# Split first loads, reassigned fill work, idle matmuls and later row sums in a fused attention and feed-forward kernel

## Chip, cores, metric

One core of one Trainium2 chip. The time is the device time of one execution in microseconds; medians are over the runs that the tables count. The engines go by their short names: PE is TensorE (PEld its weight loads), DVE VectorE, ACT ScalarE, POOL GpSimd, SP SyncE, which only issues loads and stores here. The granted clock is the share of the full clock, as a run's records give it. PE is called cold at a granted clock of 0.50, and warm at 1.00; where no clock is on record, the time of a matmul tells (a dn matmul took 548 ns in the first group of the kernel before and 349 in its long part).

## The reference

```python
# q, k, v: (8, 12, 448, 64) float32; w_in: (768, 2048); w_out: (2048, 768); alpha: (2048,)
q_n = q / sqrt(mean(q*q, -1) + 1e-6) * g_q
k_n = k / sqrt(mean(k*k, -1) + 1e-6) * g_k
attn = softmax(q_n @ k_n^T / 8)
x = (attn @ v), heads side by side            # (3584, 768)
h = x @ w_in
out = (max(h, 0) + alpha * min(h, 0)) @ w_out # (3584, 768) float32
```

## The kernel before

Heads go through in 24 groups of four (y; three groups in each of 8 batches). The program is a list of blocks n; each makes two score tiles and their exponentials, and in some blocks also the denominators (`den`, matmul group dn), the weighted values (`attv`, av, written to xT), or the transposes (`turn`, tps, copied out to qT and kT) of a group. From block 12 on, the gaps of the blocks are filled with feed-forward work: `up` (matmuls hT, then ah on ACT, then gT on DVE) and `down` (matmuls op, then osb). In the traces of this case an engine's work runs in the order of this list (two row sums at 107.11 us run ahead of the gT that PE waits for, shown below), so where a call stands decides what it holds up. The code is abridged:

```python
def load_qk(y):
    b, i = divmod(y, G)
    for nm in "qk":
        t = ld.tile([128, 2, J, D], FP32, name="nat", tag="nat", bufs=6)
        eng = nc.scalar if y < 2 and nm == "k" else nc.sync
        for g in range(2):                       # g: half of the partitions
            eng.dma_start(out=t[ds(64 * g, 64)]..., in_=SRC[nm][b, g, :, ds(2 * i, 2)])
        nat[y, nm] = t

def square(y, nm):    # sq = nat * nat: ACT for y == 0, else POOL (1.68 us); two buffers
def reduce(y, nm):    # ss = row sums of sq: DVE, 1.08 us
def root(y):          # rr = exp(-0.5 * ln(ss / D + eps)): ACT, 0.54 us
def scale(y, nm):     # qs = nat * rr
    eng = nc.vector if y == 0 or (y < G and nm == "q") else nc.gpsimd
...
# later groups, n = 3.5 y
at(n - 6, square, y, nm); at(n - 5, reduce, y, nm); at(n - 4, root, y); at(n - 3, scale, y, nm)
...
# the fill
for nm in "qk":
    square(0, nm); reduce(0, nm); root(0, nm); scale(0, nm)
turn(0)
for y in (1, 2):
    for nm in "qk":
        square(y, nm)
        at(0, reduce, y, nm) if y == 2 else reduce(y, nm)
at(1, root, 1); at(2, root, 2)
for nm in "qk":
    at(1, scale, 1, nm); at(2, scale, 2, nm)
load_v(0)
for c in range(4):
    at(2, load_w_in, c)
...
for n in range(NB + 2):
    for f, a in prep.get(n, ()):      # what at() put there: the front of the block
        f(*a)
    # scores; den or attv; exponentials; turn; the gap's ups and downs
```

Of the kernel before, what the change touches and what calls it, by code (L numbers as in the profile page):

```python
# [9 lines left out]
FP32 = mybir.dt.float32  # L10
FP16 = mybir.dt.float16
# [10 lines left out]
def kernel(  # L22
# [12 lines left out]
    nc = tc.nc  # L35

    B, H, S, D = q.shape
# [4 lines left out]
    G = HH // 2  # L42
# [7 lines left out]
    cst = ctx.enter_context(tc.tile_pool(name="cst", bufs=1))  # L50
# [5 lines left out]
    psf = ctx.enter_context(tc.tile_pool(name="psf", bufs=2, space=bass.MemoryType.PSUM))  # L56
# [15 lines left out]
    nc.vector.memset(ones, 1.0)  # L72
    ident = cst.tile([128, 128], FP16, name="ident", tag="ident")
    make_identity(nc, ident)
    gain = cst.tile([128, 1], FP32, name="gain", tag="gain")
    gk2 = cst.tile([128, 1], FP32, name="gk2", tag="gk2")
    alpha_sb = cst.tile([128, NF], FP32, name="alpha_sb", tag="alpha_sb")
# [8 lines left out]
    def load_qk(y):  # L86
        b, i = divmod(y, G)
        for nm in "qk":
            t = ld.tile([128, 2, J, D], FP32, name="nat", tag="nat", bufs=6)
            eng = nc.scalar if y < 2 and nm == "k" else nc.sync  # L90
            for g in range(2):
                eng.dma_start(
                    out=t[ds(64 * g, 64)].rearrange("p h j d -> p h (j d)"),
                    in_=SRC[nm][b, g, :, ds(2 * i, 2)],
                )
            nat[y, nm] = t

    def load_v(b):
        t = att.tile([128, HH, J, D], FP16, name="vt", tag="vt")
        for g in range(2):  # L100
            nc.gpsimd.dma_start(
                out=t[ds(64 * g, 64)].rearrange("p h j d -> p h (j d)"), in_=v4[b, g]
            )
        vt[b] = t

    def load_w_in(c):
        nc.gpsimd.dma_start(
            out=w_in_sb[:, :, ts(c, FB)],
            in_=moe_w_in[:, ts(c, FB)].rearrange("(k p) f -> p k f", p=128),
        )  # L110
# [8 lines left out]
    def square(y, nm):  # L119
        src = nat[y, nm].rearrange("p h j d -> p (h j d)")  # L120
        sq = ld.tile([128, 2 * J, D], FP32, name="sq", tag="sq", bufs=2)
        sqf = sq.rearrange("p n d -> p (n d)")
        if y == 0:
            nc.scalar.activation(out=sqf, in_=src, func=AF.Square)  # L124
        else:
            nc.gpsimd.tensor_mul(out=sqf, in0=src, in1=src)  # L126
        sqs[y, nm] = sq

    def reduce(y, nm):
        if nm == "q":  # L130
            ss_t[y] = ld.tile([128, 2, 2, J], FP32, name="ss", tag="ss", bufs=4)
        nc.vector.tensor_reduce(  # L132
            out=ss_t[y][:, "qk".index(nm)].rearrange("p h j -> p (h j)").unsqueeze(2),
            in_=sqs[y, nm], axis=AXIS_X, op=ALU.add,
        )

    def root(y, nms="qk"):
        n = len(nms)
        at = "qk".index(nms[0])
        if at == 0:  # L140
            rr_t[y] = ld.tile([128, 2, 2, J], FP32, name="rr", tag="rr", bufs=4)
        rr, ss = rr_t[y][:, ds(at, n)], ss_t[y][:, ds(at, n)]
        nc.scalar.activation(out=rr, in_=ss, func=AF.Ln, scale=1.0 / D, bias=epsb[:, 0:1])
        nc.scalar.activation(out=rr, in_=rr, func=AF.Exp, scale=-0.5)  # L144

    def scale(y, nm):
        t = ld.tile([128, J, 2, D], FP16, name="qs", tag="qs", bufs=4)
        eng = nc.vector if y == 0 or (y < G and nm == "q") else nc.gpsimd
        eng.tensor_mul(  # L149
            out=t.rearrange("p j h d -> p h j d"),  # L150
            in0=nat[y, nm],
            in1=rr_t[y][:, "qk".index(nm)].unsqueeze(3).broadcast_to((128, 2, J, D)),
        )
        qs[y, nm] = t

    def turn(y):

        ps = psa.tile([128, 2, 512], FP32, name="tps", tag="acc")
        tps = [
            ps[:, n, : S].bitcast(FP16).rearrange("p (j c) -> p j c", j=J)  # L160
            for n in range(2)
        ]
        for tp, nm in zip(tps, "qk"):
            for j in range(J):
                nc.tensor.transpose(  # L165
                    tp[:, j, :], qs[y, nm][:, j].rearrange("p h d -> p (h d)"), ident
                )
        for tp, nm in zip(tps, "qk"):
            t = att.tile([128, 2, J, 64], FP16, name=f"{nm}T", tag=f"{nm}T", bufs=3)
            o = t.rearrange("p g j c -> p j g c")  # L170
            i4 = tp.rearrange("p j (g c) -> p j g c", g=2)
            if nm == "q":
                nc.vector.tensor_copy(out=o, in_=i4)  # L173
            else:
                nc.vector.tensor_scalar(  # L175
                    out=o, in0=i4, scalar1=gain[:, 0:1], scalar2=None, op0=ALU.mult
                )
            qkT[y, nm] = t
# [4 lines left out]
    def score(y, j):  # L183
        qT, kT = qkT[y, "q"], qkT[y, "k"]
        sc = pss.tile([128, 2, 512], FP32, name="sc", tag="sc")
        for par in range(2):
            for g in range(2):
                nc.tensor.matmul(  # L188
                    out=sc[ds(64 * g, 64), par, :S],
                    lhsT=kT[ds(64 * par, 64), g, j, :],  # L190
                    rhs=qT[ds(64 * par, 64), g].rearrange("p j c -> p (j c)"),
                    start=True,
                    stop=True,
                )
        scs[y, j] = sc
# [24 lines left out]
    def den(y):  # L220
        dn = over_keys("dn", y, lambda g, par, j: ones[ds(64 * g, 64), :])
        rden[y] = dn

    def log(y):
        r = att.tile([128, 2, S], FP32, name="rden", tag="rden")
        nc.scalar.activation(out=r, in_=rden[y][:, :, :S], func=AF.Ln)  # L226
        rden[y] = r
# [33 lines left out]
    def down(b0, t, oh):  # L261
# [14 lines left out]
        if oh == 1:  # L276
            for half in range(2):
                bb, j = divmod(2 * t + half, J)
                nc.sync.dma_start(out=out4[b0 + bb, j], in_=o[ds(64 * half, 64)])




# [2 lines left out]
    def last(y):  # L286
        return (J * y + J - 1) // 2

    dens = {last(y) + 1: y for y in range(NG)}
    avs = {last(y) + 2: y for y in range(NG)}  # L290
    prep = {}

    def at(n, f, *a):
        prep.setdefault(max(int(n), 0), []).append((f, a))

    for y in range(G, NG):
        n = J * y / 2
        at(n - 12, load_qk, y)
        for nm in "qk":
            at(n - 6, square, y, nm)  # L300
            at(n - 5, reduce, y, nm)
        at(n - 4, root, y)
        for nm in "qk":
            at(n - 3, scale, y, nm)
    for b in range(1, B):
# [27 lines left out]
    def cost(n):  # L333
        return 0.75 + (1.35 if n in dens or n in avs else 0.0) + (0.9 if n in turns else 0.0)

    gaps = [[] for _ in range(NB + 2)]
    for b in range(B - 1):
        lo = last(G * b + G - 1) + 2
# [3 lines left out]
        n, clock, done = lo, cost(lo), 0.0  # L342
# [15 lines left out]
    load_qk(2)  # L358
    nc.sync.dma_start(out=alpha_sb, in_=moe_alpha.rearrange("(t p) -> p t", p=128))

    for nm in "qk":
        square(0, nm)
        reduce(0, nm)
        root(0, nm)
        scale(0, nm)
    nc.vector.tensor_mul(out=gain, in0=gain, in1=gk2)
    turn(0)
    for y in (1, 2):
        for nm in "qk":
            square(y, nm)  # L370
            at(0, reduce, y, nm) if y == 2 else reduce(y, nm)
    at(1, root, 1)
    at(2, root, 2)
    for nm in "qk":
        at(1, scale, 1, nm)
        at(2, scale, 2, nm)
    load_v(0)
    for c in range(4):
        at(2, load_w_in, c)
        at(8 + 2 * c, load_w_out, c)  # L380

    for n in range(NB + 2):
        for f, a in prep.get(n, ()):
            f(*a)
        tiles = [divmod(m, J) for m in (2 * n, 2 * n + 1) if m < NG * J]
        for t in tiles:
            score(*t)
        late = []
        if n in dens:
            den(dens[n])  # L390
        if n in avs:
            attv(avs[n])
        plain = n not in dens and n not in avs and n not in turns
        wait = plain and gaps[n] and gaps[n][0][0] is up
        for t in tiles[:1] if wait else tiles:
            soft(*t)
        if wait:
            late = [(soft, t) for t in tiles[1:]]
        if n in dens:
            log(dens[n])  # L400
            late = [(invert, (dens[n],))]
        if n in turns:
            turn(turns[n])
        for f, a in gaps[n]:
            f(*a)
            if f is up and late:
                for g, c in late:
                    g(*c)
                late = []
        for g, c in late:  # L410
            g(*c)
    for f, a in rest:
        f(*a)

# [29 lines left out]
```

## Time and profile before

| | before |
|---|---|
| median, 3 runs | 494.11 us (493.31 to 494.29) |
| span of the profiled run | 493.35 us (time of that run: 495.12) |
| first score's kT written / second group's kT written | 18.84 / 32.45 us |
| first full up-projection (hT after xT of batch 0) | 63.08 us |
| from there to the end | 430.27 us |

Read it as two stretches: a fill, in which engines wait for each other and for loads, and a long part, in which PE is nearly always busy. The prediction shows the lines that say so.

### The profile page before, as it was taken

To read this page: it belongs to the slowest core of one execution; us is meant where nothing else is said; L and a number is where in the kernel's file an instruction comes from. 1 tells how busy PE (TensorE), PEld (TensorE's weight loads), DVE (VectorE), ACT (ScalarE), POOL (GpSimd) and SP (SyncE) were. 2 spreads that over 40 slices of the span, in tenths; PEclk is the share of its full clock that TensorE was granted. 3 is DMA by queue.
4 is the path that set the end of the run, shared out by engine and by line. 5 is a ranking of instruction groups with operands and counts; after the bars stand their busy time and mean duration, and the time that the engine had idled before them with its cause. 6 is when DMAs were issued, how large, how long until landed. Compare 5 with 4: busy or idle time off the path is not lost.

```text
span 493.3 us, 9405 instructions
## 1 busy us (share of the span) xinstructions
PE 441.2 (89%) x4016; PEld 232.7 (47%) x4016; DVE 222.4 (45%) x312; ACT 287.4 (58%) x397; POOL 168.4 (34%) x124
## 2 busy tenths in 40 slices
PE   0447789999999999999999999999999999999995
PEld 0124344554445545554445555554445554454463
DVE  1781546534633535624633535634643543324421
ACT  2448878857675567557675566557675576523300
POOL 2696662535335325225335325325325200000000
PEclk9998799999999999999999999999999999999998
DMA  8599997317441470416341470417311110120122
GB/s 184 115 171 262 234 236 154 76 33 179 60 108 32 108 160 5 108 33 180 60 106 33 108 161 4 108 33 182 56 33 33 34 34 1 33 52 13 32 65 64
DMA packets 32186, 45.45 MB, mean 92 GB/s; under 512 B 5008, under 2 KB 28560, under 8 KB 32144
## 3 DMA queue, kind: packets, MB, share of 16 engines
q1 hardware_dynamic: 19792, 32.13, 25.2%
q0 software_dynamic: 11776, 11.80, 15.1%
q10 hardware_dynamic: 576, 0.92, 0.8%
q8 instruction: 31, 0.51, 0.5%
q14 instruction: 11, 0.09, 0.1%
HBM read 45.62 MB, written 11.01 MB: 115 GB/s over the span
## 4 chain that ended last, share of the span: by engine, by line
PE 67%; DVE 13%; ACT 12%; issue 4%; DMA 2%; POOL 1%; SPq 0%; DVEq 0%; POOLq 0%
PE op L265 29%; PE hT L248 19%; PE dn L211 7%; PE sc L188 6%; ACT ah L256 6%; PE av L211 5%; DVE gT L257 4%; ACT expT L200 4%; DVE ss L132 4%; DMA nat<-in_q_dram 2%; PE tps L165 2%; DVE qs L149 1%; DVE kT L175 1%; DVE qT L173 1%; POOL sq L126 1%
## 5 line engine op out<-in xcount | busy, mean ns | idle before, releaser
L200 ACT ACTIVATE expT<-sc,expb 128x896 f16<-128x896 f32 x168 | 160.2, 1003 | 59.1 <-PE sc L188 59.1
L248 PE MATMUL hT<-xT,w_in_sb 128*128 128x448 f16 x768 | 159.5, 352 | 13.0 <-DVE gT L257 11.9
L265 PE MATMUL op<-w_out_sb,gT 128*128 128x384 f16 x896 | 152.9, 326 | 0.2 <-DVE gT L257 0.2
L149 POOL TENSOR_TENSOR qs<-nat,rr 128x896 f16<-128x896 f32 x44 | 73.3, 1686 | 211.3 <-ACT rr L144 191.4
L256 ACT ACTIVATE ah<-hT,alpha_sb 128x448 f16<-128x448 f32 x128 | 81.3, 635 | 97.4 <-PE hT L248 96.1
L257 DVE TENSOR_TENSOR gT<-hT,ah 128x448 f16<-128x448 f32 x128 | 79.6, 624 | 108.4 <-ACT ah L256 107.8
L265 PEld LDWEIGHTS <-gT 128*128 128x128 f16 x896 | 85.0, 98 | 63.6 <-issue 10.1
L248 PEld LDWEIGHTS <-w_in_sb 128*128 128x128 f16 x768 | 72.3, 97 | 89.8 <-issue 30.1
L275 DVE COPY osb<-op 128x384 f32<-128x384 f32 x56 | 31.2, 557 | 115.3 <-PE op L265 115.3
L126 POOL TENSOR_TENSOR sq<-nat 128x896 f32<-128x896 f32 x46 | 76.3, 1678 | 12.9 <-DMA nat<-in_q_dram 8.6
L188 PE MATMUL sc<-qT,kT 64*64 64x448 f16 x672 | 53.5, 383 | 12.0 <-DVE kT L175 6.7
L132 DVE TENSOR_REDUCE ss<-sq 128x14 f32<-128x896 f32 x48 | 50.1, 1078 | 16.1 <-ACT sq L124 8.6
L165 PE MATMUL tps<-ident,qs 128*128 128x128 f16 x336 | 24.5, 227 | 20.3 <-DVE qs L149 20.3
L211 PE MATMUL dn<-expT,ones 64*64 64x448 f16 x672 | 39.8, 376 | 0.0
L211 PE MATMUL av<-expT,vt 64*64 64x448 f16 x672 | 36.4, 352 | 1.5 <-ACT rden L226 1.5
L188 PEld LDWEIGHTS <-kT 64*64 64x64 f16 x672 | 14.7, 108 | 44.8 <-issue 35.2
L239 DVE TENSOR_TENSOR xT<-av,rden 128x896 f16<-128x896 f32 x24 | 26.1, 1088 | 20.6 <-PE av L211 20.6
L165 PEld LDWEIGHTS <-qs 128*128 128x128 f16 x336 | 20.0, 101 | 28.6 <-DVE qs L149 21.0
L211 PEld LDWEIGHTS <-ones 64*64 64x64 f16 x672 | 21.5, 115 | 13.8 <-issue 1.6
L226 ACT ACTIVATE rden<-dn 128x896 f32<-128x896 f32 x24 | 22.1, 922 | 8.7 <-PE dn L211 8.7
L211 PEld LDWEIGHTS <-vt 64*64 64x64 f16 x672 | 20.3, 108 | 14.5 <-issue 2.8
L231 ACT ACTIVATE rden<-rden 128x896 f32<-128x896 f32 x24 | 22.7, 947 | 0.4
(22 smaller groups left out, 79.2 us busy)
## 6 DMA issues: line engine op xcount, KB each, us to landing
nat<-in_q_dram SPq DMA_DIRECT2D x48, 224.0 KB, 3.9
out_dram<-osb SPq DMA_DIRECT2D x56, 192.0 KB, 2.7
nat<-in_k_dram SPq DMA_DIRECT2D x44, 224.0 KB, 4.4
vt<-in_v_dram POOLq DMA_DIRECT2D x16, 336.0 KB, 5.5
w_in_sb<-in_moe_w_in_dram POOLq DMA_DIRECT2D x4, 768.0 KB, 19.8
w_out_sb<-in_moe_w_out_dram POOLq DMA_DIRECT2D x4, 768.0 KB, 17.1
nat<-in_k_dram ACTq DMA_DIRECT2D x4, 224.0 KB, 7.3
gain<-in_g_q_dram POOLq DMA_DIRECT2D x2, 0.2 KB, 5.5
```

The lines of the kernel that those rows point to most:

```text
L126: nc.gpsimd.tensor_mul(out=sqf, in0=src, in1=src)
L132: nc.vector.tensor_reduce(out=ss_t[y][:, "qk".index(nm)].rearrange("p h j -> p (h j)").unsqueeze(2), in_=sqs[y, nm], axis=AXIS_X, op=ALU.add,)
L149: eng.tensor_mul(out=t.rearrange("p j h d -> p h j d"), in0=nat[y, nm], in1=rr_t[y][:, "qk".index(nm)].unsqueeze(3).broadcast_to((128, 2, ...
L165: nc.tensor.transpose(tp[:, j, :], qs[y, nm][:, j].rearrange("p h d -> p (h d)"), ident)
L188: nc.tensor.matmul(out=sc[ds(64 * g, 64), par, :S], lhsT=kT[ds(64 * par, 64), g, j, :], rhs=qT[ds(64 * par, 64), g].rearrange("p j c -> p ...
L200: nc.scalar.activation(out=expT[y][:, j], in_=scs[y, j][:, :, :S], func=AF.Exp, scale=QK_SCALE, bias=expb[:, 0:1],)
L211: nc.tensor.matmul(out=acc[ds(64 * par, 64), g, :S], lhsT=weights(g, par, j), rhs=e[ds(64 * g, 64), j, par, :], start=(j == 0), stop=(j == ...
L248: nc.tensor.matmul(out=hT[:, :S], lhsT=w_in_sb[:, c, ts(ft, 128)], rhs=x[:, c, :], start=(c == 0), stop=(c == KM - 1),)
L256: nc.scalar.activation(out=ah, in_=hT[:, :S], func=AF.Copy, scale=alpha_sb[:, ft : ft + 1])
L257: nc.vector.tensor_max(out=gT[:, ft, ds((b & 1) * S, S)], in0=hT[:, :S], in1=ah)
L265: nc.tensor.matmul(out=op[:, :OH], lhsT=gT[:, ft, ts(t, 128)], rhs=w_out_sb[:, ft, ds(oh * OH, OH)], start=(ft == 0), stop=(ft == NF - 1),)
L275: nc.vector.tensor_copy(out=o[:, ds(oh * OH, OH)], in_=op[:, :OH])
```

## The change

Intent: shorten the fill. The first loads go out on two queues by partition half; the work of the first three groups is dealt out anew between ACT, DVE and POOL; idle matmuls on zeros are to keep PE's clock up; row sums and roots are emitted at the end of a block and not at its front, to be out of the way of the copies. The order of the fill changes too: group 0's roots come after both of its sums, and POOL issues the loads of v and w_in earlier, w_in ahead of the first block.

```diff
--- before.py
+++ after.py
@@ -72,6 +72,8 @@
     nc.vector.memset(ones, 1.0)
     ident = cst.tile([128, 128], FP16, name="ident", tag="ident")
     make_identity(nc, ident)
+    idle = cst.tile([128, S], FP16, name="idle", tag="idle")
+    nc.vector.memset(idle, 0.0)
     gain = cst.tile([128, 1], FP32, name="gain", tag="gain")
     gk2 = cst.tile([128, 1], FP32, name="gk2", tag="gk2")
     alpha_sb = cst.tile([128, NF], FP32, name="alpha_sb", tag="alpha_sb")
@@ -87,9 +89,8 @@
         b, i = divmod(y, G)
         for nm in "qk":
             t = ld.tile([128, 2, J, D], FP32, name="nat", tag="nat", bufs=6)
-            eng = nc.scalar if y < 2 and nm == "k" else nc.sync
             for g in range(2):
-                eng.dma_start(
+                (nc.scalar if y < G and g else nc.sync).dma_start(
                     out=t[ds(64 * g, 64)].rearrange("p h j d -> p h (j d)"),
                     in_=SRC[nm][b, g, :, ds(2 * i, 2)],
                 )
@@ -120,7 +121,7 @@
         src = nat[y, nm].rearrange("p h j d -> p (h j d)")
         sq = ld.tile([128, 2 * J, D], FP32, name="sq", tag="sq", bufs=2)
         sqf = sq.rearrange("p n d -> p (n d)")
-        if y == 0:
+        if y < 2:
             nc.scalar.activation(out=sqf, in_=src, func=AF.Square)
         else:
             nc.gpsimd.tensor_mul(out=sqf, in0=src, in1=src)
@@ -145,7 +146,7 @@
 
     def scale(y, nm):
         t = ld.tile([128, J, 2, D], FP16, name="qs", tag="qs", bufs=4)
-        eng = nc.vector if y == 0 or (y < G and nm == "q") else nc.gpsimd
+        eng = nc.vector if (y, nm) in ((0, "k"), (1, "q"), (1, "k")) else nc.gpsimd
         eng.tensor_mul(
             out=t.rearrange("p j h d -> p h j d"),
             in0=nat[y, nm],
@@ -278,6 +279,15 @@
                 bb, j = divmod(2 * t + half, J)
                 nc.sync.dma_start(out=out4[b0 + bb, j], in_=o[ds(64 * half, 64)])
 
+    def spin(count):
+
+        if count:
+            ps = psf.tile([128, 512], FP32, name="spin", tag="mm")
+            for _ in range(count):
+                nc.tensor.matmul(
+                    out=ps[:, :S], lhsT=ident, rhs=idle, start=True, stop=True
+                )
+
 
 
 
@@ -288,18 +298,21 @@
 
     dens = {last(y) + 1: y for y in range(NG)}
     avs = {last(y) + 2: y for y in range(NG)}
-    prep = {}
+    prep, post = {}, {}
 
     def at(n, f, *a):
         prep.setdefault(max(int(n), 0), []).append((f, a))
+
+    def after(n, f, *a):
+        post.setdefault(max(int(n), 0), []).append((f, a))
 
     for y in range(G, NG):
         n = J * y / 2
         at(n - 12, load_qk, y)
         for nm in "qk":
             at(n - 6, square, y, nm)
-            at(n - 5, reduce, y, nm)
-        at(n - 4, root, y)
+            after(n - 5, reduce, y, nm)
+        after(n - 4, root, y)
         for nm in "qk":
             at(n - 3, scale, y, nm)
     for b in range(1, B):
@@ -333,6 +346,7 @@
     def cost(n):
         return 0.75 + (1.35 if n in dens or n in avs else 0.0) + (0.9 if n in turns else 0.0)
 
+    first = last(G - 1) + 2
     gaps = [[] for _ in range(NB + 2)]
     for b in range(B - 1):
         lo = last(G * b + G - 1) + 2
@@ -358,26 +372,31 @@
     load_qk(2)
     nc.sync.dma_start(out=alpha_sb, in_=moe_alpha.rearrange("(t p) -> p t", p=128))
 
+    spin(32)
     for nm in "qk":
         square(0, nm)
         reduce(0, nm)
+    for nm in "qk":
         root(0, nm)
         scale(0, nm)
     nc.vector.tensor_mul(out=gain, in0=gain, in1=gk2)
     turn(0)
+    load_v(0)
     for y in (1, 2):
         for nm in "qk":
             square(y, nm)
-            at(0, reduce, y, nm) if y == 2 else reduce(y, nm)
-    at(1, root, 1)
-    at(2, root, 2)
+            if y == 1:
+                reduce(y, nm)
+    for c in range(4):
+        load_w_in(c)
+        at(8 + 2 * c, load_w_out, c)
+    after(0, root, 1)
     for nm in "qk":
-        at(1, scale, 1, nm)
-        at(2, scale, 2, nm)
-    load_v(0)
-    for c in range(4):
-        at(2, load_w_in, c)
-        at(8 + 2 * c, load_w_out, c)
+        after(0, scale, 1, nm)
+        after(1, reduce, 2, nm)
+    after(2, root, 2)
+    for nm in "qk":
+        after(2, scale, 2, nm)
 
     for n in range(NB + 2):
         for f, a in prep.get(n, ()):
@@ -409,6 +428,10 @@
                 late = []
         for g, c in late:
             g(*c)
+        if n < first:
+            spin(1 if not plain else 4)
+        for f, a in post.get(n, ()):
+            f(*a)
     for f, a in rest:
         f(*a)
```

## The prediction

> **What bounds the kernel now.** I read the page first (engine shares, the 40 slices), then busy time by windows, then the chain of waits in order of time from 0 to 80 us, then PE's groups by shape in short windows, then the timeline of the fill.
>
> ```profile
> PE 441.2 (89%) x4016; PEld 232.7 (47%) x4016; DVE 222.4 (45%) x312; ACT 287.4 (58%) x397; POOL 168.4 (34%) x124
> PE   0447789999999999999999999999999999999995
> ```
>
> PE is at 90% or more from the seventh slice (about 74 us) to the last; only the first six are loose. I cut the run at four events: first transpose (12.46), second head group's kT written (32.45), first full up-projection (63.08), and near the end. Columns: window, length, busy time (and count) of PE, weight loads, DVE, ACT, POOL; clock, DMA share, GB/s.
>
> ```profile
> 0.00:12.46 12.46, 0.00 (x1) 0.01 (x1) 2.42 (x6) 3.59 (x5) 3.08 (x11) 1.00 0.81 185
> 12.46:32.45 19.99, 7.36 (x56) 3.75 (x56) 17.07 (x13) 7.99 (x13) 15.72 (x13) 1.00 0.71 123
> 32.45:63.08 30.63, 22.28 (x275) 12.20 (x276) 11.95 (x13) 23.96 (x29) 18.81 (x15) 0.83 1.17 246
> 63.08:445.00 381.92, 369.86 (x3450) 193.74 (x3450) 176.61 (x257) 243.00 (x336) 130.79 (x87) 1.00 0.36 82
> ```
>
> After 63.08 PE idles 12 us in 382. That part has fixed PE work, so **the time is the moment of the first up-projection plus about 430 us**, and the change is worth what it takes off 63.08. The idle time after it is nearly all PE waiting for gT (10.7 us, 25 waits, none over 0.7).
>
> In the fill the chain of waits shows what ends last:
>
> ```profile
> 3.08 9.09 DMA nat<-in_q_dram
> ...
> 24.27 7.05 DVE qs L149 x2
> 31.32 0.54 DVE qT L173
> 31.85 0.60 DVE kT L175
> ...
> 34.78 2.44 PE dn L211 x22
> 37.23 0.02 issue
> 37.25 0.93 ACT rden L226
> ```
>
> The 7.05 us are two scalings that take 1.09 each when alone: DVE stood behind POOL. The dn line is slow matmuls in front of ACT.
>
> [...] The same 28 matmuls, first before 36.87 (where no clock is on record and the column's 1.00 means nothing) and then after:
>
> ```profile
> L211 PE MATMUL dn<-expT,ones 64*64 64x448 f16 x28 | 2.7, 548 | 0.0
> L211 PE MATMUL av<-expT,vt 64*64 64x448 f16 x28 | 1.5, 351 | 0.6 <-ACT rden L226 0.6
> ```
>
> ```profile
> 36.87:43.69 6.82, 4.00 (x70) 2.42 (x66) 2.31 (x3) 5.89 (x8) 2.21 (x2) 1.00 1.16 272
> 43.69:47.11 3.42, 3.42 (x40) 1.76 (x40) 0.00 (x0) 1.91 (x2) 3.42 (x3) 0.50 1.21 231
> 47.11:53.93 6.82, 3.91 (x62) 2.19 (x54) 4.20 (x5) 6.52 (x9) 2.93 (x4) 1.00 1.17 260
> 53.93:60.76 6.83, 5.78 (x60) 3.12 (x64) 1.72 (x2) 4.98 (x7) 6.83 (x5) 0.50 1.21 219
> ```
>
> Each stretch is a multiple of 3.41. [...] a scaling beside POOL took 2.59 and, of the 7.05, 4.57. [...] In the windows of 1 us the first loads move 262 GB/s at 3 to 4 us and 199 to 242 at 5 to 10 us, so another queue finds the engines busy (share 0.9 to 1.1).
>
> **Part 1, loads by half.** The records of DMA landings show the first two transfers (q0's and k0's first halves) landed at 5.3 and 4.4, the second halves at 8.5 and 8.2; then pairs about every 2 us. With the split, q0 is the first pair (5.3) and k0 the second (8.5). But there is a new wait: the loads share eight semaphores in rotation, and ACT now issues group 2's halves, the last of which waits for k0's second half. [...] its first square cannot start before about 8.5 plus one issue of 0.63, or **9.15, later than today's 8.62**. The q half that arrives early is not used early.
>
> **Part 2, fill work reassigned, to the first kT.** From 9.15: two squares at 0.94 on ACT end at 10.1 and 11.0; row sums (1.08) at 11.2 and 12.3; roots (0.54) at 11.75 and 12.85. POOL scales q 11.75 to 13.45 (1.69). DVE wants k at 12.85, [...] ends 14.45. Transposes 0.95, the two copies 1.25: kT at 16.65 against 18.85. **2.2 us earlier**, because the q and k chains overlap.
>
> **Part 3, to the second kT.** Group 1's squares are done on ACT by 15. DVE sums them 16.65 to 18.75. ACT: two exponentials, then root 1, to 19.55. POOL squares group 2 from 17.7 (two sq buffers: it waits for q1's sum) to 21.1, then issues w_in until 24.45. DVE's scaling of q1 [...] ends 22.1; k1 meets the w_in issues (today the scaling beside them took 2.56, that is 1.47 of wait), ends 24.65. Then group 2's sums, which stand before the copies in DVE's order, to 26.8; copies to 28.05. Against 32.45 that is **4.4 us in all**, 2.2 more than before.
>
> **Part 4, idle matmuls, and the attention of batch 0.** The 32 at the start are 448 columns each: 0.373 cold, 0.19 warm (from the 548 and 351 rows: 28 in four overlapping tiles take 2.7 cold and 1.35 warm); they end at about 10, inside the DMA wait, and cost nothing. The 24 others sit in the blocks before the first up-projection: four in blocks 0, 1, 3 and 10, one in eight others. PE has little to do from about 21.5 to 28, its transposes wait for DVE, so I expect it cold at 28.05. Block 3 then puts four idle matmuls, 1.5 us, ahead of the next scores. By hand from 28.05, with exponentials at 0.95, log and inverse 0.93 and 0.95, dn and av 1.32 warm, roots 0.54: all warm, ACT is the bound and the first up-projection comes 25.9 after kT. Check of this method: adding today's cold dn (3 times 1.3) and the sums in front of a copy (about 1.1) gives 30.9; measured 30.63. With a cold start of this stretch (idle matmuls and cold dn: 2.1 later) and perhaps one fall of the clock at the turn of block 6 (0.3), it is 28.3. So **2.3 saved here**, and the first up-projection at 56.4 instead of 63.08: 6.7 us.
>
> **Part 5, row sums late.** For later groups the sums move from the front of a block to its end, so in DVE's order simply one block on. Today they lie before the stalls at 114.07 (0.63), 130.50 (0.70) and 151.36 (0.19) in each 111 us. One block on they precede a block of three up-projections, where gT would come about 0.6 us later, and one with a turn and three, about 0.7. I count 0.6 worse or better in a period: 0, at most 2 us either way; I take 0.3 lost.
>
> **Sum:** 494.1 - 6.7 + 0.3 = 487.7; I say 487.0, leaning a little to a warmer PE.
>
> **Rivals.** (a) PE stays warm from the first idle matmuls[...]: kT 1.5 earlier, then 25.9 rather than 28.3: 3.9 more, 483. [...] Against: the idle PE before 28 is long against a 3.4 us window[...]. (b) The ACT queue's wait bites harder, k0 landing at 9 or later, and idle matmuls run cold ahead of real ones: the fill gains only 3, 491. For: the landing at 8.5 was the slowest of 16 engines' shares. (c) DMA becomes the bound of the fill: the share is 1.1 to 1.2 from 26 to 80 us. w_in was issued at 27.8 and its last quarter landed at 56.5; now issued from 21.1, with some 5.6 MB ahead at 265 GB/s, it lands by 43, before 56. I hold this for unlikely. (d) The sums one block later cost PE 2 us: 489.
>
> **Range and chances.** Faster by over 2% needs a gain of 9.9 us: rival (a) nearly whole, or half of it with a gain in the long part. I give 0.22. Slower needs several things not seen: 0.01. The range 482 to 491.5 spans (a) to (b).
>
> **What would show it.** First ACT square at 9.2 (wrong: under 8); kT of group 0 at 16.7, of group 1 at 28; two row sums just before that copy; the first dn at over 500 ns a matmul and the next two near 350; first up-projection at 56; PE idle from there to 445 us some 12 us as today. Wrong if squares start at 6 because the halves land sooner, if dn is warm from the first, or if idle time in the long part changes by over 3 us.

At the marks, passages are cut. The sum: 494.1, less 2.2 to the first kT, 2.2 more to the second and 2.3 after it, plus 0.3, is 487.7, and 487.0 was said. DVE's scaling of k was held up until 13.35 (0.5 us) and that of q1 until 21.0 (1.45 us), beside POOL's work. These waits are estimates from the trace before, where a scaling that takes 1.09 alone took 2.59 beside POOL's squares (14.02 to 16.61) and 4.57 beside its scalings. Rival (a)'s 1.5 us is k1's scaling without the 1.47 us of wait. That matmuls on zeros bring up the clock was not shown at the time (the last section has the runs that show it).

The numbers of what is told in part 1: in the trace before, the loads of SP and ACT carry the semaphores 101 to 108 and then 101 again; the first load on 101 landed at 5.31 and the second was issued at 5.33. Of the 16 updates that end the load of 8.53, the one before the last came at 8.03. That ACT's first square stands behind its own last issue is seen in the change: it started at 9.33, after the issue at 8.68 (0.60 us), though q0 had landed at 4.94.

## The result, and the profile after

| | before | after |
|---|---|---|
| median of the shared rounds | 494.2 us (4 runs) | 489.06 us (4 runs: 488.26 to 490.82) |
| ratio | | 0.9899 (95%: 0.9861 to 0.9937) |
| first ACT square starts | 8.62 | 9.33 |
| kT of group 0 / group 1 written | 18.84 / 32.45 | 16.95 / 26.40 |
| dn of batch 0's three groups, ns a matmul | 548, 577, 576 | 349, 349, 349 |
| first full up-projection | 63.08 | 53.25 |
| from there to the end | 430.27 | 433.29 |

A ratio is the mean time of one kernel's fast runs over that of the other's in the same rounds, so not quite the ratio of the medians. The change gains 1%: a fill that is 9.8 us shorter in the profiled runs, and a long part that is 3.0 us longer. The 9.8 is flattered, since it sets a long run of the kernel before (495.12) against one of the two short ones of the kernel after (488.30; the others 488.26, 489.81, 490.82). From the medians the fill is 7.5 to 8.2 us shorter (an estimate: the medians' difference, with before at 493.5 or 494.2, plus the 3.0).

The page of the kernel after, span and slices:

```profile
span 486.5 us, 9510 instructions
PE   6768799999999899999999899999999899999995
```

PE is now busy from the first slice on, partly with zeros. Note the slices with an 8 in the long part; before they were all 9. Busy time by windows, cut at the same events as in the prediction (window, length, busy time and count of PE, weight loads, DVE, ACT, POOL; clock, DMA share, GB/s):

```profile
0.00:13.82 13.82, 8.01 (x33) 3.55 (x33) 3.31 (x7) 4.95 (x9) 4.71 (x12) 0.93 0.79 200
13.82:26.40 12.58, 9.01 (x65) 3.78 (x65) 10.52 (x12) 8.04 (x12) 8.22 (x9) 0.67 0.98 167
26.40:53.25 26.85, 20.66 (x290) 10.63 (x291) 9.59 (x12) 24.34 (x30) 21.01 (x16) 1.00 1.18 244
53.25:445.00 391.75, 375.34 (x3483) 196.66 (x3483) 181.48 (x263) 247.05 (x340) 132.78 (x89) 1.00 0.36 82
```

The middle stretch fell from 19.99 to 12.58 us, the next from 30.63 to 26.85. In the last one ACT is busy 24.3 of 26.9 us, the most of all engines; but it does not bound this stretch alone, for the chain of waits runs through ACT for 11.4 us of it, through DVE for 8.5 and through PE for 6.4. In the long part PE's idle time is 16.4 us in 391.8, where it was 12.1 in 381.9. (Counted over equal work, up to 40 us before the end, it is 16.4 against 12.6. That is 0.8 more than the stretch grew; the difference lies in PE's busy time and was not traced.)

The chain of waits after, second kT and first denominators (start, length, what):

```profile
20.08 2.13 issue
22.21 1.08 DVE qs L150
23.29 1.99 DVE ss L133 x2
25.28 0.53 DVE qT L174
...
26.84 0.86 PE spin L287 x4
27.70 0.34 PE sc L189 x4
28.05 0.03 issue
28.07 1.90 ACT expT L201 x2
29.97 0.82 ACT rden L227
```

The 7.05 us of DVE's scalings are gone: the first takes 2.25 beside POOL's square (20.04 to 22.29; the square ended at 21.34), the second takes 1.08. Two row sums then hold up the copies, as predicted. dn (2.44 us in this place before) is no longer in the chain: it is done while ACT still makes exponentials, and the log follows ACT's own work. Block 3's four idle matmuls (spin) now stand in it with 0.86 us. PE's groups by shape, in the window 26.4 to 52 us, say why:

```profile
L212 PE MATMUL dn<-expT,ones 64*64 64x448 f16 x84 | 4.5, 349 | 0.0
```

And windows of 3.41 us show where the clock came up:

```profile
15.26:18.68 3.42, 2.11 (x16) 0.70 (x14) 2.95 (x4) 1.03 (x2) 0.66 (x1) 0.50 1.05 182
18.68:22.09 3.41, 3.41 (x19) 0.84 (x18) 2.30 (x2) 3.20 (x5) 3.41 (x3) 0.50 1.19 237
22.09:25.50 3.41, 2.07 (x27) 1.08 (x27) 3.41 (x5) 2.09 (x3) 2.54 (x4) 1.00 0.96 144
```

From 18.68 to 22.09 PE has no hole: at half clock the idle matmuls of blocks 0 and 1 and the scores fill it. Then the clock is at 1.00 until 486.3.

The long part, from PE's list of waits between 64 and 445 us (total, times, longest), before:

```profile
PE hT L248 <- DVE gT L257: 10.7, 25, 0.7
```

and after:

```profile
PE hT L249 <- DVE gT L258: 14.7, 25, 1.4
```

The same number of waits, but longer ones. One of them, DVE's timeline at 107 to 111 us:

```profile
107.11 2.07 DVE L133 TENSOR_REDUCE ss<-sq 128x14 f32<-128x896 f32 x2
109.10 1.26 DVE L258 TENSOR_TENSOR gT<-hT,ah 128x448 f16<-128x448 f32 x2
```

and PE's at the same time:

```profile
109.76 1.29 PE L249 MATMUL hT<-xT,w_in_sb 128*128 128x448 f16 x6 [1.02 <-DVE gT L258]
```

Two row sums stand ahead of gT, the third up-projection needs the buffer that gT frees, and PE waits 1.02 us. Reading the trace wait by wait, there are ten over 0.9 us after the first full up-projection: six of 1.02 (blocks with three ups and nothing else) and four of 1.36 (a turn and three ups), 11.55 us together. The kernel before has none over 0.9.

### The profile page after: what moved, and what is told of

The parts are those of the page before. It is cut to its first block, busy times and chain, and to the rows that moved or that the text cites. A ratio compares the mean times of both kernels' runs of the same rounds, so it can differ in the third digit from the quotient of the medians.

```text
span 486.5 us, 9510 instructions
## 1 busy us (share of the span) xinstructions
PE 448.4 (92%) x4072; PEld 234.3 (48%) x4072; DVE 216.7 (45%) x312; ACT 290.7 (60%) x399; POOL 166.7 (34%) x123
## 3 DMA queue, kind: packets, MB, share of 16 engines
q10 hardware_dynamic: 864, 1.38, 1.0%
## 4 chain that ended last, share of the span: by engine, by line
PE 71%; DVE 13%; ACT 11%; DMA 2%; issue 2%; POOL 0%; DVEq 0%
PE op L266 31%; PE hT L249 20%; PE sc L189 6%; PE dn L212 6%; DVE ss L133 5%; DVE gT L258 5%; ACT ah L257 5%; PE av L212 5%; ACT expT L201 4%; PE tps L166 3%; DMA nat<-in_q_dram 2%; ACT rden L232 1%; DVE kT L176 1%; DVE qT L174 1%; ACT rden L227 1%
## 5 line engine op out<-in xcount | busy, mean ns | idle before, releaser
L150 POOL TENSOR_TENSOR qs<-nat,rr 128x896 f16<-128x896 f32 x45 | 75.0, 1686 | 221.6 <-ACT rr L145 211.8
L127 POOL TENSOR_TENSOR sq<-nat 128x896 f32<-128x896 f32 x44 | 72.9, 1676 | 3.0 <-DVE ss L133 3.0
L189 PE MATMUL sc<-qT,kT 64*64 64x448 f16 x672 | 50.2, 367 | 7.5 <-DVE kT L176 5.8
L212 PE MATMUL dn<-expT,ones 64*64 64x448 f16 x672 | 35.9, 349 | 0.0
L189 PEld LDWEIGHTS <-kT 64*64 64x64 f16 x672 | 13.4, 105 | 38.6 <-issue 30.2
L212 PEld LDWEIGHTS <-ones 64*64 64x64 f16 x672 | 19.9, 107 | 11.8 <-issue 0.3
```

What stands on the lines that cost most here:

```text
L127: nc.gpsimd.tensor_mul(out=sqf, in0=src, in1=src)
L150: eng.tensor_mul(out=t.rearrange("p j h d -> p h j d"), in0=nat[y, nm], in1=rr_t[y][:, "qk".index(nm)].unsqueeze(3).broadcast_to((128, 2, ...
L189: nc.tensor.matmul(out=sc[ds(64 * g, 64), par, :S], lhsT=kT[ds(64 * par, 64), g, j, :], rhs=qT[ds(64 * par, 64), g].rearrange("p j c -> p ...
L212: nc.tensor.matmul(out=acc[ds(64 * par, 64), g, :S], lhsT=weights(g, par, j), rhs=e[ds(64 * g, 64), j, par, :], start=(j == 0), stop=(j == ...
```

## The experiments

Theory at this point: the reassigned work and the clock shorten the fill, the moved sums take 3 us back, the split loads give nothing. The rival for the 3 us was a cause beside a faster fill (landings, clock); the rivals for the fill were that one part did it all. Kernels of one batch (e1 to e4, e5 to e8, e9 to e12) ran on one chip with shared runs of the kernel before. All were correct. The events are each run's profiled execution; the median is over 4 to 6 runs, 5 rounds.

| run | median | ratio to before | second kT | first full up | to the end | dn, ns (3 groups) |
|---|---|---|---|---|---|---|
| before (medians of the batches) | 493.5 to 493.7 | 1 | 32.45 | 63.08 | 430.27 | 548, 577, 576 |
| after | 489.06 | 0.9899 | 26.40 | 53.25 | 433.29 | 349, 349, 349 |
| e1 sums in front | 486.71 | 0.9856 | 26.59 | 55.06 | 430.22 | 424, 349, 349 |
| e2 before, late sums only | 496.26 | 1.0051 | 31.51 | 60.34 | 433.31 | 575, 349, 349 |
| e3 no idle matmuls | 489.98 | 0.9929 | 26.87 | 56.27 | 433.30 | 576, 438, 457 |
| e4 sums at the denominators | 483.01 | 0.9787 | 25.97 | 54.06 | 426.52 | 385, 349, 349 |
| e5 loads by tensor | 488.99 | 0.9910 | 25.69 | 52.54 | 433.31 | 349, 349, 349 |
| e6 work as before | 493.99 | 1.0012 | 29.78 | 58.98 | 433.31 | 577, 349, 349 |
| e7 no first 32 | 489.16 | 0.9913 | 26.15 | 55.68 | 433.32 | 576, 570, 349 |
| e8 before, idle only | 493.35 | 1.0005 | 32.65 | 61.23 | 430.27 | 416, 349, 349 |
| e9 e4 and e5 together | 482.62 | 0.9774 | 25.40 | 53.56 | 426.55 | 398, 349, 349 |
| e10 e9, idle in the turns | 481.51 | 0.9747 | 25.92 | 52.98 | 426.57 | 349, 349, 349 |
| e11 reassigned work only | 487.82 | 0.9869 | 26.04 | 55.78 | 430.26 | 575, 574, 525 |
| e12 e10 without the first 32 | 481.38 | 0.9747 | 25.99 | 53.05 | 426.53 | 349, 349, 349 |

The length of the long part repeats to 0.1 us and takes just three values, by where the sums stand. The fill varies by a few us with the clock (first full up-projection at 53.25 in the change, with every dn at 349 ns, and at 55.68 in e7, with two at 576 and 570, though the medians are 489.06 and 489.16), so single profiled fills are to be compared with care: the one of before is 1.4 to 1.7 us longer than its medians tell.

### e1: the sums back in front

```diff
-            after(n - 5, reduce, y, nm)
-        after(n - 4, root, y)
+            at(n - 5, reduce, y, nm)
+        at(n - 4, root, y)
```

> The changed kernel with only the row sums and roots of groups 3 and later put back to the front of their blocks. Theory: the long part lost 3 us because the sums, one block later, stand ahead of gT where three up-projections follow (waits of 1.02 and 1.36 us, ten of them). Then those ten waits go back to what they were, PE's idle time from the first full up-projection to 445 us falls from about 17 to about 12 to 13 us, the first up-projection stays within 1.5 us of 53.3, and the time is about 486 (3 below the changed kernel). Rival: the long part is longer for another cause (weights or groups landing later beside a faster fill, or the clock); then the time stays at 489.

Measured: 486.71 us; the long part 430.22, PE's waits between 64 and 445 us those of before, and none over 0.9 left:

```profile
PE hT L249 <- DVE gT L258: 10.4, 25, 0.7
```

So the moved sums are the whole 3 us, and the rival falls: the second kT comes as early as in the change (26.59), and the long part is back to 430.2. (The roots moved with the sums and were not tried alone; in the timeline above it is the sums that stand ahead of gT.) One thing expected failed: the first up-projection was to stay within 1.5 us of 53.3, and came at 55.06, after a fall of the clock (below).

### e2: late sums alone, on the kernel before

The same edit the other way round, with `post` emitted at each block's end.

> The kernel before with only the sums and roots of groups 3 and later emitted at the end of their blocks. Theory: ten waits of 1.0 to 1.4 us for gT come up, the long part grows by about 3 us, the fill changes by under 1.5 us: 496 to 497. Rival (the change's own intent): sums at the end of a block are out of the way of the copies and the time falls to about 492.

Measured: 496.26 us, 2.7 us above the median of before in the same batch (493.55), with a long part of 433.31 and the same ten waits (11.54 us). Its profiled fill was 2.7 us shorter, where under 1.5 was expected; the clock was at 1.00 from 38.4 on in that run and did not fall again (0.999 in the mean). But that run (495.43) was the fastest but one of its six, and the fill that it is compared with is that of the long run of before. By the medians nothing is left of it: 2.7 us longer in all, 3.0 of them in the long part. Alone, this part of the change makes the kernel slower.

### e3: no idle matmuls

```diff
-    spin(32)
-        if n < first:
-            spin(1 if not plain else 4)
```

> The changed kernel without any idle matmul. Theory: the clock is half until about 35 us or later and falls again as in the kernel before, the first dn takes about 550 ns a matmul, each cold dn is 1.3 us ahead of ACT; the first full up-projection comes 2.5 to 4 us later (56 to 57) and the time is about 492. Rival: the reassigned work alone shortened the fill, the idle matmuls only fill holes: first up-projection at 53 to 54, time 489.

Measured: in the profiled run the first up-projection at 56.27 and cold dn (576, 438, 457), as expected; but the median is 489.98, only 0.9 us above the change's 489.06, where I expected 3. The runs' granted clocks explain it from both sides. The change's four runs took 488.30, 490.82, 488.26 and 489.81 us at 0.989, 0.986, 0.989 and 0.986: the longer two have 0.003 less of the clock, about what one more window of 3.41 us at 0.50 takes (an estimate: 0.5 x 3.41 / 488 is 0.0035). The profiled one, with every dn warm, was a lucky one. Of e3's six runs the profiled one was the slowest (491.37 at 0.991; the five others 489.68 to 490.11 at 0.998 and 0.999), so its 56.27 and its cold dn are not typical either. The idle matmuls of the change are worth about 1 us and not 3, and the intervals of the two ratios (0.9861 to 0.9937, 0.9916 to 0.9942) don't tell even that from nothing.

### e4: the sums where PE is busy with denominators

```diff
-            at(n - 6, square, y, nm)
-            after(n - 5, reduce, y, nm)
-        after(n - 4, root, y)
+            at(n - 6 if y < 5 else n - 8, square, y, nm)
+            if y < 5:
+                after(n - 5, reduce, y, nm)
+            else:
+                at(last(y - 3) + 1, reduce, y, nm)      # the block of den(y - 3)
+        after(n - 4 if y < 5 else last(y - 3) + 1, root, y)
```

> The changed kernel with the sums of groups 5 and later at the front of the block that holds the denominators of the third group before (their squares two blocks earlier, their root at the end of that block). There 28 dn matmuls, 1.5 us, stand on PE between the scores and the first up-projection, so by hand two sums (2.1 us) are done before the first gT can start. Theory: the ten waits of 1.02 and 1.36 us shrink to the 0.4 to 0.5 that ACT causes anyway, PE's idle time in the long part falls from 17 to about 10 us, time about 482. Rival: two sums cost gT the same wherever they stand, the waits move to the denominators' blocks, time 487 to 489.

Measured: 483.01 us, and a long part of 426.52, 6.8 us below the change's and 3.7 below the kernel before. PE's waits between 64 and 445 us:

```profile
PE hT L249 <- DVE gT L258: 9.5, 27, 0.8
```

No wait over 0.9 is left (the longest are five of 0.80, where 0.4 to 0.5 was expected; nearly all others are 0.25), and PE's idle time after the first full up-projection (up to 40 us before the end) is 9.65 us, where the change has 16.41 and the kernel before 12.55. The cost of a sum is not fixed: it is what stands behind it on DVE when PE needs it.

### e5: the first loads by tensor

```diff
-                (nc.scalar if y < G and g else nc.sync).dma_start(
+                (nc.scalar if y < 2 and nm == "k" else nc.sync).dma_start(
```

> The changed kernel with the first loads back on the queues of before (q on SP, k of groups 0 and 1 on ACT). Theory: the split is not used early, since ACT must issue group 2's halves after k0's second half has landed and before its first square; without it the first square starts at about 8.6 instead of 9.3 and the first kT comes 0.3 to 0.9 us earlier, time 488 to 489, no worse than the change. Rival: the split speeds up the loads; without it the first square is later than 9.5 or the first kT later than 17.3, time 490 or more.

Measured: the first square at 8.63 (9.33 with the split), second kT at 25.69 (26.40), the median the same (488.99). The split has no gain. The 0.7 us is that of two single runs: over all profiled runs the first square starts at 8.64 to 9.80 with the split (six runs) and at 8.33 to 8.97 without (eight), as the loads land. Its cost is seen on ACT's timeline of the kernel after, where the last load that ACT issues waits for k's second half (landed at 8.66 by the landing records) and the square behind it:

```profile
4.96 0.60 ACTq L93 DMA_DIRECT2D nat<-in_q_dram  x1
8.68 0.60 ACTq L93 DMA_DIRECT2D nat<-in_k_dram  x1
9.33 0.95 ACT L125 ACTIVATE sq<-nat 128x896 f32<-128x896 f32 x1 [5.88 <-DMA nat<-in_k_dram]
```

q0's halves had landed at 4.1 and 4.9 (landing records) and lay there until 9.33.

### e6: the fill's work dealt out as before

```diff
-        if y < 2:
+        if y == 0:
-        eng = nc.vector if (y, nm) in ((0, "k"), (1, "q"), (1, "k")) else nc.gpsimd
+        eng = nc.vector if y == 0 or (y < G and nm == "q") else nc.gpsimd
```

> The changed kernel with the squares of group 1 back on POOL and the scalings back on DVE and POOL as before (all else as changed: the order of roots, idle matmuls, late sums). Theory: DVE and POOL stand in each other's way as before: group 1's squares occupy POOL ahead of group 2's, the second kT comes 2 to 4 us later than 26.4, first up-projection at 55 to 57, time 491 to 493. Rival: the overlap of the q and k chains and the warm clock did it all; second kT at 26 to 27, time 489.

Measured: 493.99 us, no faster than the kernel before; second kT at 29.78 instead of 26.40, with the first dn cold again. The second kT is as late as expected; the first up-projection (58.98, expected 55 to 57) and the time (491 to 493) are worse. On POOL's timeline of this run group 1's k is scaled only after the w_in issues:

```profile
22.47 3.36 POOL L108 DMA_DIRECT2D w_in_sb<-in_moe_w_in_dram  x4
25.81 3.38 POOL L150 TENSOR_TENSOR qs<-nat,rr 128x896 f16<-128x896 f32 x2
```

With the change both of group 1's scalings are DVE's and ended at 23.29. So without the reassignment the rest of the change gives nothing in sum: its fill is still shorter than that of before (58.98 against 63.08; by the medians about 2.5 us, an estimate), and the late sums take the 3.0 back. Nor is e6 the old work in the old order: the new order puts the w_in issues, 3.36 us, ahead of k's scaling on POOL, which the kernel before did not. The old assignment with w_in issued at block 2, and the new order alone, were not tried.

### e7 and e8: parts of the idle matmuls

e7 is the change without `spin(32)`; e8 is the kernel before with `idle`, `spin(32)` and the blocks' `spin` added.

> The changed kernel without the 32 idle matmuls at the start (the 24 in the blocks stay). Theory: they are for nothing, since the clock falls again at 11.85 before the first real matmul; the four in block 0 and four in block 1 fill the window that sets the clock up at about 22. Then the clock is half until about 22 and the first up-projection and the time stay (53.3, 489). Rival: the first 32 carry the clock; the first dn is cold and the time is 1 to 3 us longer.

> The kernel before with only the idle matmuls added. Theory: they fill windows in which PE waits, the clock stays full through more of the fill, each dn that was cold (three at 1.3 us on the path) becomes warm: first up-projection at about 60 to 61 instead of 63.1, time 491 to 492. Rival: [...] PE goes cold again and block 3's four idle matmuls stand ahead of real ones: first up-projection at 62.5 or later, time 494.

Measured, e7: 489.16, the same as the change. The theory holds for the time, but not for the events: in the profiled run the clock, up at 20.67, fell again at 27.49 and the first two dn were cold. The same program without the 32 can be lucky or not; so can the one with them. e7's six runs say the same: 488.25 and 488.76 at a granted clock of 0.999, 490.77 (the profiled one) and 490.05 at 0.992. e8: 493.35 against 493.47 for before in the same batch: no gain. The first up-projection of the profiled run came 1.85 us earlier, nearly as the theory had it, but that is no gain: this run (493.27) is like its median, and the run of before that it is set against took 495.12, just 1.85 more. The theory's 491 to 492 did not come.

That pointed at the phase. By the clock's records its windows begin at another moment in each run (first change at 5.02 in the change's profiled run, 6.36 in e1, 5.43 in e4). In e1 the window after the clock came up held the hole in block 2, between the transposes and the copies:

```profile
23.42:26.84 3.42, 1.46 (x22) 0.87 (x20) 3.17 (x5) 2.62 (x5) 2.03 (x3) 1.00 1.14 155
26.84:30.25 3.41, 3.41 (x28) 1.31 (x28) 0.00 (x0) 2.13 (x4) 3.41 (x3) 0.50 1.10 235
```

PE was busy 1.46 of 3.42 us, the clock fell, and the first dn was partly cold (424). In the change's profiled run the same hole lay in a window with 2.07 of 3.41 us busy, and the clock held.

### e9 to e12: putting it together

e9 is e4 with e5's loads. e10 adds:

```diff
-            spin(1 if not plain else 4)
+            spin(7 if n in turns else 4 if plain else 1)
```

e12 is e10 without `spin(32)`. e11 is the change with e5's loads, e1's sums and no idle matmuls: the reassigned work alone.

> The sums at the denominators' blocks together with the first loads back by tensor. Theory: the two gains add: long part 426.5 as with the sums alone, second kT at 25.7 instead of 26.0 to 26.4, first up-projection at 53 to 55 as the clock's phase falls, time 482 to 483. Rival: the earlier start only shifts the clock's windows and nothing is left of it: 483 to 484.

> As the run before it, with seven idle matmuls instead of one after the transposes of blocks 2, 6 and 9, where PE waits 1 to 2 us for DVE's copies. Theory: what differs from run to run in the fill is whether a window of 3.41 us falls on the hole of block 2; filled, the clock stays full from about 22 us in every phase, first dn at 349, first up-projection at 52.5 to 53.5, time about 481.5 and a narrower spread. Rival: idle matmuls stand ahead of real ones and cost what they save; time 483.

> The changed kernel without its idle matmuls, with sums in front and loads by tensor: of the change only the reassigned work is left. Theory: that is the part that pays: second kT at 25.7 to 26.9, long part 430.3, first up-projection at 55.5 to 57, time 486.5 to 488, which is below the whole change. Rival: the parts need each other, and alone it gives 490 or more.

> As the run with seven idle matmuls in the turn blocks, without the 32 at the start. Theory: the 32 change nothing, since the clock falls before the first real matmul is done; the time stays within 0.7 us of that run. Rival: they matter for the phase or for the first transposes and scores: 1 us or more slower.

Measured: e9 482.62, within its theory's 482 to 483, but only 0.4 us below e4 (483.01, on another chip; the intervals of the ratios overlap), so the loads give at most some tenths. e10 481.51: the first dn is warm, and the five runs lie within 1.0 us, all of them below e9's fastest (481.98). e12 481.38, its four runs within 0.07 us (481.33 to 481.40); the change's four spread over 2.6. In e12 the window that was the hole in e1 is 76% busy, and the clock holds:

```profile
22.82:26.24 3.42, 2.60 (x28) 1.42 (x26) 3.17 (x5) 2.63 (x5) 2.03 (x3) 1.00 1.08 153
```

The first 32 idle matmuls do nothing that the time shows, as expected. e11 took 487.82: the fill's work, reassigned and reordered, is alone worth 1.3% (0.9869, 95%: 0.9849 to 0.9889), at least about as much as the whole change (0.9899, 0.9861 to 0.9937).

e12 is faster than the kernel before, 0.9747 of it (95%: 0.9731 to 0.9764). It shared no round with the change, whose ratio is 1.5 points higher, with an interval well clear of this one.

## Why the prediction was right and wrong

The time, 489.06 against 487.0, is in the range, and "within 2%" was the outcome that it gave the best chance. But two terms of its sum were off, in opposite directions, so that the sum came so close is luck. Two of the three signs that it gave for being wrong came true: dn was warm from the first, and PE's idle time up to 445 us rose from 12.1 to 16.4. There is a slip at its start as well: the events that it counts from are those of a run of 495.12 us, and it takes what they give off 494.1.

- **Loads.** Right. First square at 9.15 predicted, 9.33 measured, held up by the ACT queue's own wait; e5 shows that nothing is lost without the split. (Its reading of the DMA engines as busy left out the window from 4 to 5 us: 153 GB/s, share 0.73.)
- **First kT.** Right: 16.65 predicted, 16.95 measured (15.95 to 17.42 in the runs that keep the change's dealing-out).
- **Second kT.** 28.05 predicted, 26.40 measured. The term that failed is the 1.47 us that k1's scaling was to stand beside the w_in issues: it waited not at all (22.21 to 23.29). From first to second kT it is 9.45 us in the change and in all runs that keep its dealing-out, so this is no luck of one run. The two row sums ahead of the copies came as told.
- **Idle matmuls and clock.** The prediction counted 28.3 us from second kT to first up-projection, for a cold PE; the profiled run had 26.85, with every dn at 349. The step that failed is "PE has little to do from about 21.5 to 28, [...] so I expect it cold": I did not see that at half clock the idle matmuls and scores fill the window to 22.09 completely. Its reading of when the clock falls was also off: the single windows before the two falls were busy 1.59 and 1.58 of 3.41 us, 46 to 47%, while the stretches of two windows that it read were busy 4.00 and 3.91 of 6.82, 59 and 57%. It depends on the phase, though: in e1, where the clock fell at 26.84, the same stretch took 28.47 (55.06 less 26.59). The all-warm 25.9 was itself 0.95 short; the row sums of group 3 stand ahead of a copy in that chain (33.56 to 35.55), which I had not counted, and those of group 4 (45.22, 2.00 us) ahead of a root that ACT waits for; so ACT is not "the bound".
- **Late sums.** Mechanism and places right, sum wrong: 0.3 us predicted, 3.0 measured. The single waits were well sized: 0.6 and 0.7 expected on top of what was there, 0.63 (1.02 against 0.39) and 0.85 (1.36 against 0.51) measured. But in 111 us there are two blocks of the first kind and one of the second, which is 2.1 us, and the old waits in exchange shrank by only 0.9 (0.63 to 0.25, 0.70 to 0.34, 0.19 to nothing). I set gain against loss as equal without counting the blocks. e1 and e2 show the 3.0, from both sides.
- **Rivals.** (a), in the profiled run (3.1 of its 3.9 us), and (d) both came true and nearly cancelled. (b) did not. (c) did not bind, but nearly: I had w_in's last quarter land by 43; by the landing records it was 50.5, with the first up-projection at 53.25 waiting for xT.

What stays open: why a DVE scaling beside the w_in issues took 2.56 us in the kernel before and 1.08 in the change, when both began 0.06 to 0.08 us into the second issue (the 2.56 repeats in e2 and e8, the 1.08 in all ten runs with the change's dealing-out); and what the new order of the fill is worth without the new assignment.

## What to carry to other kernels

Where an engine's work runs in program order, as in these traces (two row sums at 107.11 us ran ahead of gT, and PE waited 1.02 us), moving an instruction does not take it off the path; ask what stands behind it and when that is needed, and put it where the busy engine has other work (here beside the denominators: 6.8 us between two places for the same sums). When a change has several parts, undo each: here the fill's reassigned and reordered work carried the gain, the late sums took 3 us of it back, the idle matmuls gave about 1 us if anything, and the split loads nothing. Look also at how long the profiled run itself took: the one of before was long and the one of the change short, and by their profiles alone the fill seems to gain some 2 us more than it does. Where the clock's records follow the load, as here (in e1 the clock fell after a window busy for 1.46 of 3.42 us; in e12, with that hole filled to 2.60, it held), fill the longest hole and judge by the spread of runs (2.6 us in the change, 0.07 in e12), not by one profile.

## What the runs show of the clock, and of DVE beside POOL

- The clock fell after windows in which PE was by no means idle: 1.46 of 3.42 us busy in e1, 1.38 of 3.41 in e9, 1.88 in e11 (from 44.59 us). It held at 2.07 of 3.41 (the change), 2.60 of 3.42 (e12), and even 1.43 (e2, from 41.83 us). So no single share parts these runs: the clock fell after 1.88 and held after 1.43.
- Matmuls on zeros brought the clock up: in the change it first came up at 5.02 us, after a window (1.61 to 5.02) in which PE ran nothing but idle matmuls, 3.41 of 3.41 us (one started every 0.373 us before, every 0.19 after). In e12 it came up at 22.82, after windows that idle matmuls helped to fill, and in e3, which has none, not before 33.35 (its first dn took 576 ns a matmul).
- A scaling on DVE took longer beside POOL's multiplications: 1.08 or 1.09 alone, 2.25 beside POOL's square in the change, 2.59 beside its squares and 4.57 beside its scalings in the kernel before. Beside the w_in issues it took 1.08 in the change and 2.56 in the kernel before, e2 and e8; what makes the difference was not shown.
